# Attention sums and values as 64-row matmuls in the two column halves of the array

## Chip, cores, metric

The kernel runs on one core of one Trainium2 chip. The metric is device time in microseconds (us) from one execution, median of several. All comparisons below are between runs of the fast state; one execution of the changed kernel fell in a slow one (314.56 us at a mean granted TensorE clock of 0.982, against 0.998 to 1.0) and is left out.

## The reference

Pooled attention, then a feed-forward layer with g = h cos h. Cut to what matters:

```python
# q, k, v: (8, 8, 576, 64); keys and values are averaged over groups of 8 positions
k_p, v_p = k.reshape(B, H, 72, 8, D).mean(3), v.reshape(B, H, 72, 8, D).mean(3)
attn = np.exp(scale * q @ k_p.T - max)
out = (attn / attn.sum(-1)) @ v_p                 # (8, 8, 576, 64)
x = out.transpose(0, 2, 1, 3).reshape(4608, 512)  # tokens x (heads * 64)
h = x @ w_in                                      # 512 -> 2048
return (h * np.cos(h)) @ w_out                    # 2048 -> 512
```

## The kernel before

The feed-forward layer runs in nine stages of 512 tokens: an up stage (L297, 64 matmuls of 128x128 weights on 512 columns) and a down stage (L310, 64 more). The attention of the next batch is sprinkled into the down stage as units: scores (`scores_mm`, L211, then Exp, L218) and later values. A large unit is four heads by 256 queries, a small one (`REST`) eight heads by 64. The keys are pooled to 72, so the contraction of values and sums is over 72 rows.

```python
    banks = [psum.tile([128, 2, 512], FP32, name=f"bank{i}") for i in range(3)]     # two PSUM banks each
    obanks = [psum.tile([128, 512], FP32, name=f"obank{i}") for i in range(2)]
    ...
    def values(b, u, pair, later=None):
        (c0, n), (h0, nh) = u
        ex = att.pop(("ex", b, u))
        for i in range(nh):
            pj, hp = divmod(h0 + i, 2)
            # vz holds [v of the even head, 8s, 8s, v of the odd head], 64 columns each:
            # one matmul of 128 output rows gives values in one half and sums in the other
            nc.tensor.matmul(pair[:, hp, (i // 2) * n:(i // 2 + 1) * n],                      # L241
                             lhsT=vz[b % 2][:, pj, 2 * hp:2 * hp + 2, :].rearrange("p a d -> p (a d)"),
                             rhs=ex[:, ex_col(u, i):ex_col(u, i) + n])
        w = nh * n // 2
        lnc, inv = inverse_tile(w)
        for hp in range(2):
            nc.scalar.activation(out=lnc[half[1 - hp]], in_=pair[half[1 - hp], hp, 0:w], func=ACTF.Ln)   # L247
        nc.scalar.activation(out=inv, in_=lnc, func=ACTF.Exp, scale=-1.0)                     # L248
        def mul():
            for hp in range(2):
                nc.vector.tensor_mul(out=x_out(b, u, half[hp]), in0=cols(pair[half[hp], hp, :], u),   # L252
                                     in1=cols(inv[half[1 - hp]], u))
        ...
    # in the stage loop, for stages 1 to 6: (before which down matmul of 64, what)
            fill = [(4, scores_of((b, us[0], 2), (b, us[1], 0))), (14, V_(0, 1, later)), (16, lambda: later.pop()()),
                    (19, V_(1, 2)), (35, scores_of((b, us[2], 0), (b, us[3], 1), (t, REST, 2))),
                    (38, V_(2, 0)), (43, lambda: values(t, REST, banks[1])), (46, V_(3, 2))]
```

The prologue (batch 0) already uses `sums_first` (L266) and `values_then` (L280), which run 64-row matmuls in the column halves; the change brings that form to the steady stages.

The softmax here doesn't subtract the row's maximum and nothing guards it: scores larger than these inputs give would overflow.

## Time and profile before

| | before |
|---|---|
| time, median | 302.38 us (302.17 to 302.52, 3 runs) |
| TensorE busy | 293.9 of 301.4 us |
| ScalarE (ACT), VectorE (DVE) busy | 205.7, 170.8 us |
| one steady stage, first L297 matmul to that of the next stage | 31.30 us |

"Busy" for TensorE says little by itself, since ends of matmuls are modelled. What carries the argument is the time from the start of one group of matmuls to the start of the next, read from the timeline. The prediction below shows the lines.

### The profile page before, as it was taken

Reading aid. Unit: us, or ns where it says so; the run is one execution under the profiler, and the core shown is the slowest. Engines: PE = TensorE matmul, PEld = TensorE weight load, DVE = VectorE, ACT = ScalarE, POOL = GpSimd, SP = SyncE. Lnnn points to the kernel's source line nnn. Section 1 sums busy time; section 2 is a strip of 40 time slices with the busy share of each in tenths; the row PEclk is TensorE's granted clock in tenths of the full one; section 3 lists DMA queues with packets and bytes.
Section 4 is the critical chain, followed back from the end, with each engine's and each line's share of the span. In section 5 each row is a group of like instructions: output and inputs, shape, how many; then the busy total and the mean of one; then the engine's idle time right before and its main releaser. Section 6 shows DMA issues by size and latency. Waiting matters only on the chain.

```text
span 301.4 us, 4625 instructions
## 1 busy us (share of the span) xinstructions
PE 293.9 (97%) x1816; PEld 143.2 (48%) x1816; DVE 170.8 (57%) x212; ACT 205.7 (68%) x254; POOL 130.4 (43%) x93
## 2 busy tenths in 40 slices
PE   8789999999999999999999999999999999999995
PEld 3445544445544454445444544455444544444444
DVE  5448637465467446754666556654775477425712
ACT  3786798469876987688778886789668966605500
POOL 8463016984983398239913990389300000000000
PEclk9999999999999999999999999999999999999999
DMA  7999999639526961697079617791811130131023
GB/s 152 197 207 206 206 205 195 141 55 176 117 60 124 167 127 29 146 158 140 6 170 143 129 36 171 94 174 39 141 32 35 37 70 0 37 70 35 0 67 75
DMA packets 44165, 32.91 MB, mean 109 GB/s; under 512 B 22128, under 2 KB 39408, under 8 KB 44144
## 3 DMA queue, kind: packets, MB, share of 16 engines
q0 software_dynamic: 19744, 18.07, 38.3%
q1 hardware_dynamic: 24160, 14.42, 20.5%
q8 instruction: 14, 0.23, 0.3%
q10 hardware_dynamic: 240, 0.13, 0.2%
q14 instruction: 7, 0.06, 0.1%
HBM read 36.70 MB, written 9.44 MB: 153 GB/s over the span
## 4 chain that ended last, share of the span: by engine, by line
PE 93%; DMA 4%; POOL 1%; DVE 1%; issue 0%; POOLq 0%; DVEq 0%
PE bank L297 41%; PE obank L310 41%; PE bank L241 5%; DMA kv_st<-in_v_dram 4%; PE bank L211 3%; PE bank L328 1%; PE bank L165 1%; POOL q_b L84 1%; PE obank L157 0%; PE obank L280 0%; PE obank L192 0%; DVE xT L282 0%; DVE vz L167 0%; POOL kv_st L84 0%; DVE o_sb L316 0%
## 5 line engine op out<-in xcount | busy, mean ns | idle before, releaser
L310 PE MATMUL obank<-w_out_sb,g_sb 128*128 128x512 bf16 x560 | 131.4, 379 | 0.0
L297 PE MATMUL bank<-xT,w_in_sb 128*128 128x512 bf16 x576 | 126.6, 379 | 0.0
L304 ACT ACTIVATE cos<-bank,half_pi 128x1024 f32<-128x1024 f32 x72 | 79.3, 1113 | 59.5 <-PE bank L297 59.5
L307 DVE TENSOR_TENSOR g_sb<-bank,cos 128x1024 bf16<-128x1024 f32 x72 | 87.3, 1223 | 43.0 <-ACT cos L304 42.9
L297 PEld LDWEIGHTS <-w_in_sb 128*128 128x128 bf16 x576 | 56.1, 98 | 67.6 <-issue 1.6
L310 PEld LDWEIGHTS <-g_sb 128*128 128x128 bf16 x560 | 52.8, 98 | 56.5 <-issue 2.0
L252 DVE TENSOR_TENSOR xT<-bank,inv 64x512 bf16<-64x512 f32 (+1 forms) x72 | 45.3, 629 | 40.8 <-ACT inv L248 40.1
L141 POOL TENSOR_TENSOR kv_st<-kv_st 72x2048 f32<-72x2048 bf16 x12 | 48.7, 4058 | 33.9 <-DMA kv_st<-in_k_dram 33.9
L247 ACT ACTIVATE lnc<-bank 64x512 f32<-64x512 f32 (+1 forms) x72 | 39.2, 544 | 3.1 <-PE bank L241 1.7
L316 DVE COPY o_sb<-obank 128x512 f32<-128x512 f32 x35 | 23.6, 689 | 30.9 <-PE obank L310 30.5
L218 ACT ACTIVATE ex<-bank 72x1024 bf16<-72x1024 f32 (+1 forms) x40 | 35.0, 929 | 8.5 <-PE bank L211 8.4
L142 POOL TENSOR_TENSOR kv_st<-kv_st 72x1024 f32<-72x1024 f32 x12 | 28.2, 2349 | 1.0
L248 ACT ACTIVATE inv<-lnc 128x512 f32<-128x512 f32 (+1 forms) x36 | 21.0, 583 | 1.1
L241 PE MATMUL bank<-ex,vz 72*128 72x256 bf16 (+1 forms) x176 | 20.0, 243 | 0.0
L241 PEld LDWEIGHTS <-vz 72*128 72x128 bf16 x176 | 13.6, 97 | 9.6 <-DVE xT L252 0.5
L145 POOL TENSOR_TENSOR kp<-kv_st 72x512 bf16<-72x512 f32 x12 | 14.9, 1263 | 0.5
L211 PE MATMUL bank<-qT,kk 64*72 64x256 bf16 (+1 forms) x192 | 13.2, 252 | 0.0
L211 PEld LDWEIGHTS <-kk 64*72 64x72 bf16 x192 | 7.4, 109 | 9.9 <-issue 7.2
L285 ACT ACT_TABLE_LOAD x9 | 11.5, 1283 | 0.9 <-PEq L519 0.7
L499 POOL COPY gate<-kk 1x1 bf16<-1x1 bf16 x5 | 0.9, 179 | 25.7 <-DMA kk<-kp 25.7
L288 ACT ACT_TABLE_LOAD x9 | 11.5, 1283 | 0.2
L103 POOL DMA_DIRECT2D kv_st<-in_v_dram x6 | 5.0, 841 | 8.8 <-PE bank L165 8.8
(55 smaller groups left out, 93.1 us busy)
## 6 DMA issues: line engine op xcount, KB each, us to landing
out_dram<-o_sb SPq DMA_DIRECT2D x70, 128.0 KB, 2.4
kv_st<-in_v_dram POOLq DMA_DIRECT2D x8, 576.0 KB, 13.7
kv_st<-in_k_dram POOLq DMA_DIRECT2D x7, 576.0 KB, 7.6
q_b<-in_q_dram POOLq DMA_DIRECT2D x6, 576.0 KB, 9.9
w_in_sb<-in_moe_w_in_dram POOLq DMA_DIRECT2D x4, 512.0 KB, 14.5
w_out_sb<-in_moe_w_out_dram POOLq DMA_DIRECT2D x4, 512.0 KB, 18.1
q_b<-in_q_dram POOLq DMA_DIRECT2D x4, 288.0 KB, 13.0
g_sb<-in_k_dram SPq DMA_DIRECT2D x1, 576.0 KB, 3.7
```

The source lines that it names most:

```text
L141: add(out=s, in0=x[:, :, 0:4, :], in1=x[:, :, 4:8, :], op=ADD)
L142: add(out=s[:, :, 0:2, :], in0=s[:, :, 0:2, :], in1=s[:, :, 2:4, :], op=ADD)
L211: nc.tensor.matmul(pair[:Sp, bank, c:c + n].rearrange("p (g n) -> p g n", n=64), lhsT=kk[b % 2][half[r], h0 + i, 0:Sp], rhs=att["qT", b][h ...
L218: nc.scalar.activation(out=ex[:, 0:nh * n].rearrange("p (a n) -> p a n", a=2), in_=pair[:Sp, :, 0:nh * n // 2], func=ACTF.Exp, scale=scale ...
L241: nc.tensor.matmul(pair[:, hp, (i // 2) * n:(i // 2 + 1) * n], lhsT=vz[b % 2][:, pj, 2 * hp:2 * hp + 2, :].rearrange("p a d -> p (a d)"), ...
L247: nc.scalar.activation(out=lnc[half[1 - hp]], in_=pair[half[1 - hp], hp, 0:w], func=ACTF.Ln)
L252: nc.vector.tensor_mul(out=x_out(b, u, half[hp]), in0=cols(pair[half[hp], hp, :], u), in1=cols(inv[half[1 - hp]], u))
L297: nc.tensor.matmul(h[:, j, :], lhsT=w_in_sb[fc // 4][:, ki, (fc % 4) * 128:(fc % 4 + 1) * 128], rhs=xT[:, ki, t * TILE:(t + 1) * TILE], st ...
L304: nc.scalar.activation(out=cos, in_=h, func=ACTF.Sin, bias=half_pi[:, :1])
L307: nc.vector.tensor_mul(out=g_sb[:, 2 * fp:2 * fp + 2, :], in0=h, in1=cos)
L310: nc.tensor.matmul(o, lhsT=g_sb[:, fc, ms * 128:(ms + 1) * 128], rhs=w_out_sb[fc // 4][:, fc % 4, :], start=(fc == 0), stop=(fc == FFCH - 1))
L316: nc.vector.tensor_copy(out=o[:, 0:n], in_=ps)
```

## The change

The intent: let the sums of all heads of a unit lie in one bank over all 128 partitions and the values in the other, so that one Ln and one product over 128 partitions do what two of each over 64 did. For that, each head's matmul of 128 output rows becomes two of 64, and even and odd heads go side by side in the two column halves of the array. A stretch in which the matmuls use the divided array, between matmuls that use all of it, is called a visit below. Its way in is what the last full matmuls before it take beyond their pace, its way out what passes beyond the pace until the next full matmul starts.

```diff
-        for i in range(nh):
-            pj, hp = divmod(h0 + i, 2)
-            nc.tensor.matmul(pair[:, hp, (i // 2) * n:(i // 2 + 1) * n],
-                             lhsT=vz[b % 2][:, pj, 2 * hp:2 * hp + 2, :].rearrange("p a d -> p (a d)"),
-                             rhs=ex[:, ex_col(u, i):ex_col(u, i) + n])
         w = nh * n // 2
+        cs, ao = pair[:, 0, 0:w], pair[:, 1, 0:w]
+        for out_of, weights in ((cs, lambda i: ones[:Sp, :]),
+                                (ao, lambda i: vz[b % 2][:, (h0 + i) // 2, 3 * (i % 2), :])):
+            for i in range(nh):
+                hp = i % 2
+                nc.tensor.matmul(out_of[hp * 64:hp * 64 + 64, (i // 2) * n:(i // 2 + 1) * n], lhsT=weights(i),
+                                 rhs=ex[:, ex_col(u, i):ex_col(u, i) + n])
         lnc, inv = inverse_tile(w)
-        for hp in range(2):
-            nc.scalar.activation(out=lnc[half[1 - hp]], in_=pair[half[1 - hp], hp, 0:w], func=ACTF.Ln)
+        nc.scalar.activation(out=lnc, in_=cs, func=ACTF.Ln)
         nc.scalar.activation(out=inv, in_=lnc, func=ACTF.Exp, scale=-1.0)
 
         def mul():
-            for hp in range(2):
-                nc.vector.tensor_mul(out=x_out(b, u, half[hp]), in0=cols(pair[half[hp], hp, :], u),
-                                     in1=cols(inv[half[1 - hp]], u))
+            nc.vector.tensor_mul(out=x_out(b, u, slice(0, 128)), in0=cols(ao, u), in1=cols(inv, u))
```

## The prediction

> **What bounds the kernel now.** I read the page first: engines, slices, the chain that ended last.
>
> ```profile
> PE 293.9 (97%) x1816; PEld 143.2 (48%) x1816; DVE 170.8 (57%) x212; ACT 205.7 (68%) x254; POOL 130.4 (43%) x93
> PE 93%; DMA 4%; POOL 1%; DVE 1%; issue 0%; POOLq 0%; DVEq 0%
> ```
>
> TensorE is busy 97% of the 301.4 us span and the chain lies on it for 93%. Busy matmul time alone proves little, so I asked next whether TensorE ever waits for what the change makes cheaper: the logarithm (L247, ACT) and the products (L252, DVE). From the list of waits:
>
> ```profile
> PEld L211 <- DVE xT L252: 1.9, 7, 0.4
> ...
> PEld L241 <- DVE xT L252: 0.5, 1, 0.5
> ```
>
> (The columns are total us, times and longest.) Nobody waits for L247. The 1.9 us are seven times 0.27 us in front of the scores, and the third view shows that this is no wait for data. It is TensorE's timeline in a steady stage; the first column is the start, and I use differences of starts only, since the ends are modelled:
>
> ```profile
> 99.14 1.03 PE L310 MATMUL obank<-w_out_sb,g_sb 128*128 128x512 bf16 x4
> 100.09 0.63 PE L211 MATMUL bank<-qT,kk 64*72 64x256 bf16 x8
> 100.65 2.33 PE L310 MATMUL obank<-w_out_sb,g_sb 128*128 128x512 bf16 x10
> 102.83 0.60 PE L241 MATMUL bank<-ex,vz 72*128 72x256 bf16 x4
> 103.27 1.25 PE L310 MATMUL obank<-w_out_sb,g_sb 128*128 128x512 bf16 x5
> 104.35 0.60 PE L241 MATMUL bank<-ex,vz 72*128 72x256 bf16 x4
> ```
>
> Five L310 matmuls take 104.35 - 103.27 = 1.08 us, 0.216 each: TensorE's pace with no gap. Four of L241 take 0.44 us, 0.109 each, and the five after them lose nothing: a unit of values is free of any transition. The scores (L211), which use half arrays of 64 rows, are not: the four L310 ahead take 0.95 instead of 0.864 (0.09 lost), the eight scores in four pairs take 0.56 against 4 x 0.107 = 0.43 of streaming (0.13 lost), and the ten after them take 2.18 against 2.16 (some 0.01 to 0.02). That is 0.23 to 0.24 us per visit to a divided array. So a steady stage is TensorE's instruction stream end to end (in the chain of waits its pieces join without holes from 99.30 to 130.59), and what counts is only what the change does to that stream.
>
> **What the Trainium skill says.** "TensorEngine Tiling (Array Packing)", section Key Properties: changing the tiling mode, not merely the tile, drains TensorE. The trace agrees, with the 0.09 us in and some 0.1 us out around L211. The same page, section Restrictions under the tile-to-partition mapping: column tiling disables the fast weight load. In the trace a 72x64 weight load takes 109 ns (L280) and a 72x128 one 97 ns (L241), so the half as wide one is the slower; it overlaps matmuls all the same. "TensorE: Matmul & The Clock Gate", section Back-to-back issue gap: 262 cycles for 256 columns, 109 ns at 2.4 GHz; the trace has 0.109. "Trainium Kernel Development and Optimization", Performance Expectations, says that matmul busy time is a bad metric because matmuls are pipelined; hence the differences of starts.
>
> **The change, part by part.** `values` is used only in the loop: per batch four units of 4 heads x 256 columns for batches 1 to 7, and one of 8 heads x 64 for batches 0 to 7. That is 28 large units (112 matmuls of 256) and 8 small ones (64 of 64), as the groups by form count L241.
>
> Removed: one Ln and one product per unit.
>
> ```profile
> L252 DVE TENSOR_TENSOR xT<-bank,inv 64x512 bf16<-64x512 f32 x56 | 38.6, 689 | 38.9 <-ACT inv L248 38.4
> L247 ACT ACTIVATE lnc<-bank 64x512 f32<-64x512 f32 x56 | 33.1, 592 | 1.8 <-PE bank L241 0.7
> L252 DVE TENSOR_TENSOR xT<-bank,inv 64x256 bf16<-64x256 f32 x16 | 6.8, 422 | 1.9 <-ACT inv L248 1.6
> L247 ACT ACTIVATE lnc<-bank 64x256 f32<-64x256 f32 x16 | 6.1, 379 | 1.4 <-PE bank L241 1.0
> L282 DVE TENSOR_TENSOR xT<-obank,inv 128x512 bf16<-128x512 f32 x3 | 2.0, 688 | 0.6 <-PE obank L280 0.6
> L270 ACT ACTIVATE lnc<-obank 128x512 f32<-128x512 f32 x2 | 1.2, 597 | 0.0
> ```
>
> The last two rows, from the prologue, are the new forms: 128 partitions cost what 64 do. So ACT loses 28 x 0.592 + 8 x 0.379 = 19.6 us (205.7 to 186) and DVE 28 x 0.689 + 8 x 0.422 = 22.7 us (170.8 to 148). All of it lies beside TensorE.
>
> Added: L241's 176 matmuls become 352 of 64 output rows, two at a time in the two column halves. The prologue already runs this very form (L266, L280). Eight L280 matmuls from 16.52 to the next matmul of the same mode at 16.98 take 0.46 us, four pairs at 0.109 and 0.024 for the first pair. So the streaming of a large unit stays the same: 4 x 0.109 before, four pairs of 0.109 after. What is new is the mode, 128x64, between L310 matmuls in 128x128. Its way out is measured:
>
> ```profile
> 12.19 0.41 PE L266 MATMUL obank<-ex,ones 72*64 72x256 bf16 x4 [0.15 <-DVE kk L132]
> 12.54 0.61 PE L392 MATMUL bank<-warm 128*128 128x512 bf16 x2
> ```
>
> Two pairs to the first 128x128 matmul in 0.34 us, of which 0.213 stream: 0.13 for the first pair and the way out, the same as with L211 (four in 0.34 at 39.34 us). The way in from 128x128 never stands without a data wait in front of it; from the row mode it is 0.09 (L165's last start at 15.42, L266 at 15.61, less 0.109), as is L211's. I take 0.09.
>
> Large unit: 0.09 in + 0.13 first pair and out + 0.015 in the next matmul - 0.01 that it loses now = 0.224 us. Times 28: **6.3 us**.
>
> Small unit: now eight matmuls in 0.23 us (111.38 to 111.61). After, eight pairs of 64 columns. The nearest form is L157, 36 pairs of 72 columns in 64x64 tiles:
>
> ```profile
> 27.14 1.36 PE L157 MATMUL obank<-groups,kv_st 64*64 64x72 bf16 x72
> 28.43 0.39 PE L297 MATMUL bank<-xT,w_in_sb 128*128 128x512 bf16 x1
> ```
>
> (1.29 - 0.12) / 36 = 0.0325 us a pair. So 8 x 0.0325 + 0.12 + 0.09 + 0.015 - 0.23 = 0.25 us, times 8: **2.0 us**.
>
> Given back: in the first stage eight L310 before the values at 48.37 us take 0.20 us more than their pace, the one 0.5 us wait on L252; the shorter products should end it: -0.2. And the first small unit follows the pooling of V, whose mode change is paid already: -0.1.
>
> Sum: 302.4 + 6.3 + 2.0 - 0.3 = **310.4 us**, 2.6% slower.
>
> **The rivals.** *The relief of ACT and DVE shortens it.* For: ACT is busy about 15.7 of 17.45 us in a steady down stage, and some 42 us of work vanish. Against: no engine waits for L247, TensorE waits once for L252, and the up stage (64 matmuls in 13.85 us) runs at TensorE's own pace. At most the 0.2 us above, if entering the mode were free as well: 302.
>
> *Only half of the switch is paid*, because K stays 72 rows and the weights of the halves could be loaded ahead while the full array still streams: no 0.09 on the way in, 36 x 0.09 = 3.2 us less: 307. For: a full-width load runs ahead of the matmul in flight (the 97 ns loads cost L241 nothing). Against: L211's loads start only with its matmuls.
>
> *The two halves' weight loads do not overlap.* In the small units 16 loads in sequence at some 0.06 a pair add 8 x 8 x 0.03 = 1.8 us: 312. Against: in L157 two 64-column loads fit in 0.0325 us, though there in different rows of the array as well, which is why it stays open. In the large units 0.109 a pair hides them, as L280 shows.
>
> **Range and chances.** The 2.6% stand on one number taken 36 times, 0.22 to 0.25 us, three quarters of it measured in this form. Half a switch gives the low end with what is between, serial loads the high end: 307.9 to 312.2. The line of 2% is at 308.4; below it lies the rival with a free way in and a part of the spread. Faster by over 2%: 0.01; within 2%: 0.17; slower: 0.82.
>
> **What would show it.** In the changed profile: ACT near 186 and DVE near 148 us; no new wait of TensorE for ACT or DVE; L310 ahead of the values late by 0.09 us and the unit itself at 0.56 us instead of 0.44 to the next L310; small units near 0.38 to the next L310; up stages unchanged at 13.85 us; steady iterations longer by 4 x 0.224 + 0.25 = 1.15 us. Wrong if the L310 run ahead of the values loses nothing, if pairs start more than 0.109 us apart, or if stages shorten anywhere but at 48 us.

## The result, and the profile after

The changed kernel takes 309.8 us (median of its five executions; the four fast ones are 309.53 to 309.86, median 309.69) against 302.52 us (302.17 to 302.7, 5 runs): ratio 1.0237, 95% interval 1.0223 to 1.0252. It is slower. Ratios here and below are the mean time of one kernel's fast runs over that of the other's of the same rounds, so not quite the ratio of the medians.

The run `after_again` repeats the changed kernel on another chip and gives a fast profile:

> The changed kernel once more, for a profile of the fast state. My theory: 309.7 us as before; the profile's steady stage is 1.04 us longer than that of the kernel before, made up of five visits to the divided array at 0.22 to 0.25 us each, less 0.1 us because the scores of the last unit no longer wait for the product (L252) that frees their bank.

Measured: 309.61 us (309.33 to 309.89), ratio 1.0241 (1.0223 to 1.026). Its lines are numbered differently: L245 are the matmuls of sums and values, L248 the Ln, L249 the Exp, L252 the product, L309 the down matmuls, L296 the up matmuls. The engines on its page:

```profile
PE 300.6 (98%) x1992; PEld 141.4 (46%) x1992; DVE 148.2 (48%) x176; ACT 185.1 (60%) x218; POOL 130.4 (42%) x93
```

ACT lost 20.6 and DVE 22.6 us, as intended. TensorE's busy time grew by 6.7 us, but since ends are modelled, the starts have to say where. Its timeline in a steady stage (columns: start, length, engine, line, operation):

```profile
99.99 1.03 PE L309 MATMUL obank<-w_out_sb,g_sb 128*128 128x512 bf16 x4
100.95 0.63 PE L211 MATMUL bank<-qT,kk 64*72 64x256 bf16 x8
101.51 2.33 PE L309 MATMUL obank<-w_out_sb,g_sb 128*128 128x512 bf16 x10
103.77 0.41 PE L245 MATMUL bank<-ex,ones 72*64 72x256 bf16 x4
104.01 0.39 PE L245 MATMUL bank<-ex,vz 72*64 72x256 bf16 x4
104.33 1.25 PE L309 MATMUL obank<-w_out_sb,g_sb 128*128 128x512 bf16 x5
105.51 0.41 PE L245 MATMUL bank<-ex,ones 72*64 72x256 bf16 x4
```

Ten L309 now take 2.26 instead of 2.18 us, which is the way in (0.08), and five take 1.18 instead of 1.08, the way in of the next visit and 0.01 to 0.02 left from the one before. The unit itself takes 0.56 from its start (103.77) to the next L309 (104.33) instead of 0.44. The weight-load row shows the same from the other side. In the list of waits (us in total, times, longest):

```profile
PEld L245 <- issue: 15.0, 36, 0.4
```

Thirty-six units, and in front of each the weight loads stand still for some 0.4 us: the first load for the divided array starts with the unit's first matmul (both at 103.77 us) and not ahead of it. L241's loads, before, were idle this way 0.2 us once.

Where the time went, by stages of these two profiles (each from the first up matmul to the next stage's, or in the first stage from the first down matmul; precise starts of the trace):

| | before | changed | difference | predicted |
|---|---|---|---|---|
| down stage 0 | 19.37 | 20.54, of it 0.36 waiting for the load of w_out | 0.80 without that wait | 0.85 |
| stages 1 to 6, each | 31.297 | 32.330 | 1.033, times 6: 6.20 | 1.15, times 6: 6.9 |
| stage 7 (one small unit) | 28.258 | 28.498 | 0.24 | 0.25 |
| stage 8 and the end | 31.40 | 31.39 | 0.0 | 0.0 |

Without that wait the stages lose 7.2 us together; the medians differ by 7.3.

The 0.36 us are a matter of the start: that execution reached its first up matmul 1.34 us earlier than the one of before (17.04 against 18.38 us) and so came to a weight matrix that was still on its way (the timeline names the load of w_out as what ended the wait). Such differences of the start move whole times by some tenths from execution to execution, which is why I compare stages where less than 1 us is at stake.

### The profile page after: what moved, and what is told of

It is laid out like the page before. It is cut to its first block, busy times and chain, and to the rows that moved or that the text cites. A ratio compares the mean times of both kernels' runs of the same rounds, so it can differ in the third digit from the quotient of the medians.

```text
span 312.8 us, 4899 instructions
## 1 busy us (share of the span) xinstructions
PE 304.6 (97%) x1992; PEld 142.7 (46%) x1992; DVE 148.2 (47%) x176; ACT 185.3 (59%) x218; POOL 130.5 (42%) x93
## 4 chain that ended last, share of the span: by engine, by line
PE 93%; DMA 3%; POOL 1%; issue 1%; DVE 0%; ACT 0%; POOLq 0%
PE bank L296 41%; PE obank L309 40%; PE bank L245 6%; DMA kv_st<-in_v_dram 3%; PE bank L211 3%; PE bank L327 1%; PE obank L279 1%; POOL q_b L84 1%; PE obank L157 0%; PE bank L165 0%; PE obank L192 0%; ACT ex L218 0%; DVE vz L167 0%; POOL kv_st L84 0%; PE bank L265 0%
## 5 line engine op out<-in xcount | busy, mean ns | idle before, releaser
L309 PE MATMUL obank<-w_out_sb,g_sb 128*128 128x512 bf16 x560 | 131.7, 380 | 0.0
L296 PE MATMUL bank<-xT,w_in_sb 128*128 128x512 bf16 x576 | 128.9, 384 | 0.0
L296 PEld LDWEIGHTS <-w_in_sb 128*128 128x128 bf16 x576 | 56.6, 99 | 69.5 <-issue 4.8
L309 PEld LDWEIGHTS <-g_sb 128*128 128x128 bf16 x560 | 50.4, 98 | 61.7 <-issue 7.5
L252 DVE TENSOR_TENSOR xT<-bank,inv 128x512 bf16<-128x512 f32 (+1 forms) x36 | 22.8, 632 | 43.5 <-ACT inv L249 43.1
L248 ACT ACTIVATE lnc<-bank 128x512 f32<-128x512 f32 (+1 forms) x36 | 19.8, 549 | 8.8 <-PE bank L245 8.4
L249 ACT ACTIVATE inv<-lnc 128x512 f32<-128x512 f32 (+1 forms) x36 | 21.0, 583 | 1.1
L245 PE MATMUL bank<-ex,ones 72*64 72x256 bf16 (+1 forms) x176 | 14.0, 253 | 0.0
L245 PE MATMUL bank<-ex,vz 72*64 72x256 bf16 (+1 forms) x176 | 13.3, 245 | 0.0
L245 PEld LDWEIGHTS <-ones 72*64 72x64 bf16 x176 | 6.0, 108 | 15.0 <-issue 15.0
L211 PE MATMUL bank<-qT,kk 64*72 64x256 bf16 (+1 forms) x192 | 12.1, 250 | 0.0
L211 PEld LDWEIGHTS <-kk 64*72 64x72 bf16 x192 | 7.9, 110 | 8.5 <-issue 7.6
```

The lines of the kernel that those rows point to most:

```text
L211: nc.tensor.matmul(pair[:Sp, bank, c:c + n].rearrange("p (g n) -> p g n", n=64), lhsT=kk[b % 2][half[r], h0 + i, 0:Sp], rhs=att["qT", b][h ...
L245: nc.tensor.matmul(out_of[hp * 64:hp * 64 + 64, (i // 2) * n:(i // 2 + 1) * n], lhsT=weights(i), rhs=ex[:, ex_col(u, i):ex_col(u, i) + n])
L252: nc.vector.tensor_mul(out=x_out(b, u, slice(0, 128)), in0=cols(ao, u), in1=cols(inv, u))
L296: nc.tensor.matmul(h[:, j, :], lhsT=w_in_sb[fc // 4][:, ki, (fc % 4) * 128:(fc % 4 + 1) * 128], rhs=xT[:, ki, t * TILE:(t + 1) * TILE], st ...
L309: nc.tensor.matmul(o, lhsT=g_sb[:, fc, ms * 128:(ms + 1) * 128], rhs=w_out_sb[fc // 4][:, fc % 4, :], start=(fc == 0), stop=(fc == FFCH - 1))
```

## The experiments

**The two halves of the change, each alone.** `pe_part` makes the same number and shapes of matmuls, in pairs in the column halves, but with the old layout of banks (each pair is now the sums and the values of one head), so ACT and DVE do the old work:

```diff
-            nc.tensor.matmul(pair[:, hp, (i // 2) * n:(i // 2 + 1) * n],
-                             lhsT=vz[b % 2][:, pj, 2 * hp:2 * hp + 2, :].rearrange("p a d -> p (a d)"),
-                             rhs=ex[:, ex_col(u, i):ex_col(u, i) + n])
+            for a in range(2):
+                nc.tensor.matmul(pair[half[a], hp, (i // 2) * n:(i // 2 + 1) * n],
+                                 lhsT=vz[b % 2][:, pj, 2 * hp + a, :], rhs=ex[:, ex_col(u, i):ex_col(u, i) + n])
```

> TensorE's half of the change alone: 64-row matmuls in column halves, but laid out in the banks as before, so that two Ln and two products per unit remain. Theory (the cost is the visits): the same TensorE stream as the changed kernel, 309.5 to 310.5 us; the relief of ACT and DVE is worth at most 0.1 us a stage. Rival (the lighter ACT and DVE hide a larger TensorE cost in the changed kernel): over 312 us.

Measured: 309.26 us (309.22 to 309.37), just under the range expected, ratio 1.023 (1.0213 to 1.0248); steady stages of 32.33 us, equal to the changed kernel's. TensorE's half is the whole of the loss.

`relief_part` keeps the 128-row matmuls and takes one Ln and one product per unit. For that the weights are chosen so that the first bank holds sums in all partitions and the second values. Its output is wrong, which doesn't matter for the time.

```diff
-                             lhsT=vz[b % 2][:, pj, 2 * hp:2 * hp + 2, :].rearrange("p a d -> p (a d)"),
+                             lhsT=weights(pj, hp),        # 128 neighbouring columns of vz
...
-        for hp in range(2):
-            nc.scalar.activation(out=lnc[half[1 - hp]], in_=pair[half[1 - hp], hp, 0:w], func=ACTF.Ln)
+        nc.scalar.activation(out=lnc, in_=pair[:, 0, 0:w], func=ACTF.Ln)
...
-            for hp in range(2):
-                nc.vector.tensor_mul(out=x_out(b, u, half[hp]), in0=cols(pair[half[hp], hp, :], u),
-                                     in1=cols(inv[half[1 - hp]], u))
+            nc.vector.tensor_mul(out=x_out(b, u, slice(0, 128)), in0=cols(pair[:, 1, :], u), in1=cols(inv, u))
```

> The other half alone, wrong results on purpose: TensorE's matmuls of 128 output rows as before, but one Ln and one product per unit over 128 partitions. Theory: only the wait of the last scores for L252 goes (0.14 us in some six stages), of which 0.08 comes back as a wait for the exponential: 301.6 us, 0.2 to 0.4% faster. Rival (ACT and DVE hold TensorE up more than the waits show): below 300 us; rival (nothing at all is to be had): 302.5.

Measured: 301.96 us (301.69 to 303.09), ratio 0.9993 (0.9973 to 1.0013). The steady stage is 31.292 us against 31.297: the relief is worth nothing there. My expectation, 0.14 us a stage with 0.08 of it coming back, was wrong, and the timelines say why. The kernel before, second scores of a stage and what follows, and ACT at the same time:

```profile
108.34 0.93 PE L211 MATMUL bank<-qT,kk 64*72 64x256 bf16 x16
109.20 0.82 PE L310 MATMUL obank<-w_out_sb,g_sb 128*128 128x512 bf16 x3
109.86 0.27 PE L241 MATMUL bank<-ex,vz 72*128 72x256 bf16 x1
108.79 1.93 ACT L218 ACTIVATE ex<-bank 72x1024 bf16<-72x1024 f32 x2 [1.32 <-PE bank L211]
```

The same in `relief_part` (L312 are its down matmuls, L246 its values):

```profile
107.43 0.76 PE L211 MATMUL bank<-qT,kk 64*72 64x256 bf16 x16
108.12 0.82 PE L312 MATMUL obank<-w_out_sb,g_sb 128*128 128x512 bf16 x3
108.95 0.60 PE L246 MATMUL bank<-ex,vz 72*128 72x256 bf16 x4
107.88 1.93 ACT L218 ACTIVATE ex<-bank 72x1024 bf16<-72x1024 f32 x2 [2.48 <-PE bank L211]
```

The sixteen scores take 0.69 instead of 0.86 us to the next group: a wait of 0.17 us for L252, in front of the last eight of them, is indeed gone. But the three down matmuls now take 0.83 instead of 0.66, and the values start 1.52 us after the scores in both. They need the first exponential of those scores (the ACT line holds two, about 1 us each). It starts 0.45 us after the scores in both kernels, once the first eight are done, and so ends just before the values start. One wait lay beside another that ends at the same moment.

**What a unit pays for.** `split_visit` puts one down matmul between the sums and the values of each unit: the same instructions, twice as many visits to the divided array.

```diff
                                 (ao, lambda i: vz[b % 2][:, (h0 + i) // 2, 3 * (i % 2), :])):
+            if out_of is ao and between is not None:
+                between()
             for i in range(nh):
...              # between puts the next down matmul; the stage loop is changed to match
```

> The changed kernel with one output-projection matmul between the sums and the values of each unit: the same instructions, but two visits to the divided array per unit instead of one. Theory (each visit costs 0.22 us, in, first pair and out): 36 x 0.225 = 8.1 us more than the changed kernel, 317.8 us. Rival (the cost comes with the doubled number of matmuls and the slower weight loads): no change, 309.7 us.

Measured: 317.71 us (317.26 to 318.6), ratio 1.0513 (1.049 to 1.0536): 8.1 us above the changed kernel, 0.225 us for each of the 36 added visits. Its timeline (L311 are the down matmuls, L247 the sums and values):

```profile
105.79 0.41 PE L247 MATMUL bank<-ex,ones 72*64 72x256 bf16 x4
106.14 0.39 PE L311 MATMUL obank<-w_out_sb,g_sb 128*128 128x512 bf16 x1
106.45 0.41 PE L247 MATMUL bank<-ex,vz 72*64 72x256 bf16 x4
106.80 0.39 PE L311 MATMUL obank<-w_out_sb,g_sb 128*128 128x512 bf16 x1
```

Two pairs take 0.34 to the next L311 where 0.22 would be their pace, and one L311 takes 0.32 (precise starts) to the next group instead of 0.216: 0.22 to 0.23 for an added visit.

`tiny_visit` is the kernel before with one small pair of 64-row matmuls ahead of each unit:

```diff
         ex = att.pop(("ex", b, u))
+        for a in range(2):
+            nc.tensor.matmul(pair[half[a], 0, 0:64], lhsT=ones[:Sp, :], rhs=ex[:, 0:64])
         for i in range(nh):
```

> The kernel before with one pair of 64-column matmuls in the column halves, whose result is overwritten, ahead of the four or eight matmuls of each unit. All else is as before. Theory (a visit costs the same however little is done in it): 36 x 0.23 = 8.3 us more, less up to 0.9 us as the wait for L252 is covered: 309.9 to 310.8 us. Rival (cost by matmuls and weight loads): 72 small ones, 36 x 0.03 = 1.1 us more, 303.6 us.

Measured: 311.13 us (310.54 to 311.21), ratio 1.0282 (1.0261 to 1.0302), a little over the range expected. In the profiled execution (311.18 us) that excess is not of the visits: the stretch from the last matmul to the end is 4.51 us, against 3.72 before. No visit lies there, and why it was longer was not looked into. A pair that streams for 0.03 us costs as much as the whole change: its steady stages are 32.467 us, 1.17 above those of before, for five visits. The lines (L240 the pair, L243 the old matmuls, L312 the down matmuls):

```profile
103.99 0.22 PE L240 MATMUL bank<-ex,ones 72*64 72x64 bf16 x2
104.14 0.61 PE L243 MATMUL bank<-ex,vz 72*128 72x256 bf16 x4
104.59 1.25 PE L312 MATMUL obank<-w_out_sb,g_sb 128*128 128x512 bf16 x5
105.76 0.22 PE L240 MATMUL bank<-ex,ones 72*64 72x64 bf16 x2
```

0.15 us from the pair to the next matmul, 0.45 for the four old ones, 1.17 instead of 1.08 for the five down matmuls ahead of the next visit.

`grouped` goes the other way: the changed kernel with two visits per steady stage instead of five.

```diff
-            fill = [(4, scores_of(...)), (14, V_(0, 1, later)), (16, lambda: later.pop()()),
-                    (19, V_(1, 2)), (35, scores_of(...)),
-                    (38, V_(2, 0)), (43, lambda: values(t, REST, banks[1])), (46, V_(3, 2))]
+            fill = [(4, scores_of(...)), (19, V_(0, 1)), (19, V_(1, 2)), (35, scores_of(...)),
+                    (43, V_(2, 0)), (43, V_(3, 2)), (43, lambda: values(t, REST, banks[1]))]
```

> The changed kernel with the units of six steady stages gathered into two visits per stage instead of five (two units at the nineteenth matmul, two and the small one at the forty-third). Theory: three visits fewer in six stages, 18 x 0.224 = 4.0 us less than the changed kernel: 305.7 us, still slower than the kernel before. If the products at the stage's end come too late for the next stage, up to 0.5 us a stage comes back: up to 308.7. Rival (cost by matmuls): 309.7 us.

Measured: 305.22 us (304.28 to 305.79), ratio 1.0089 (1.0072 to 1.0107); stages of 31.57 us, 0.76 less than the changed kernel's for three visits fewer (18 visits, 4.6 us by stages, 4.4 by times of different chips). Three visits at 0.22 are 0.67; the other 0.09 is about the wait for the exponential in front of the third unit, which now comes later (the three L309 there take 0.83 in the changed kernel and 0.75 elsewhere). No product was late for the stage's end. It is the best form of the changed kernel that I ran, and still 0.9% slower than the kernel before.

**Do the halves share their time?** `halves_in_turn` was to show it by order: all matmuls of one half ahead of all of the other.

```diff
-        for out_of, weights in ((cs, ...), (ao, ...)):
-            for i in range(nh):
-                hp = i % 2
+        for hp in range(2):
+            for out_of, weights, i in [(o, f, i) for o, f in ((cs, ...), (ao, ...)) for i in range(hp, nh, 2)]:
```

> The changed kernel with all matmuls of one column half ahead of all of the other, so that only one pair in a unit can run side by side. Theory (pairs share their time): a large unit takes seven slots of 0.108 us instead of four, +0.325 us x 28 = 9.1, a small one fifteen of about 0.03 instead of eight, +0.2 us x 8 = 1.7: 320.5 us. Rival (the halves do not overlap anyway, or the order does not matter): 309.7 us.

Measured: 310.83 us (310.6 to 311.42), ratio 1.0281 (1.0263 to 1.0299): 1.2 us above the changed kernel and not 11. The expectation missed, and not because pairs gain nothing. A small unit of it, where the program has four sums and four values of the first half, then four sums and four values of the second:

```profile
113.79 0.31 PE L244 MATMUL bank<-ex,ones 72*64 72x64 bf16 x4
113.94 0.20 PE L244 MATMUL bank<-ex,vz 72*64 72x64 bf16 x1
113.94 0.22 PE L244 MATMUL bank<-ex,ones 72*64 72x64 bf16 x1
113.97 0.20 PE L244 MATMUL bank<-ex,vz 72*64 72x64 bf16 x1
114.00 0.20 PE L244 MATMUL bank<-ex,ones 72*64 72x64 bf16 x1
```

The sums of the second half start between the values of the first: they overtake matmuls that stand ahead of them in the program. The unit takes 0.524 us to the next down matmul instead of 0.374, while a large unit, with only four matmuls in a half, takes 0.570 instead of 0.560. So in this trace each half takes its matmuls in its own order, some three or four ahead, and the order of the program mattered only beyond that. 28 x 0.01 + 8 x 0.15 = 1.5 us is about what was measured.

`one_half` tests the same by place: all matmuls of a unit in the lower half. Its output is wrong, which doesn't matter for the time.

```diff
-                nc.tensor.matmul(out_of[hp * 64:hp * 64 + 64, (i // 2) * n:(i // 2 + 1) * n], lhsT=weights(i),
+                nc.tensor.matmul(out_of[half[0], (i // 2) * n:(i // 2 + 1) * n], lhsT=weights(i),
...              # Ln and Exp on half[0] alone; two products, both from half[0]
```

> The changed kernel with all of a unit's 64-row matmuls in the lower column half, wrong results on purpose; Ln, Exp and products read that half alone. It replaces the test by order, which failed because the two halves took their matmuls independently of each other. Theory (two halves share their time, one cannot): eight slots of 0.108 us instead of four in a large unit, +0.43 us x 28 = 12.1, sixteen of 0.0315 instead of eight in a small one, +0.25 us x 8 = 2.0: 309.6 + 14.1 = 323.7 us. Rival (the halves gave nothing): 309.6 us.

Measured: 323.24 us (323.16 to 323.69), ratio 1.0696 (1.0673 to 1.0718). Its unit (L310 are the down matmuls) is 0.99 us from start to the next down matmul, against 0.56:

```profile
107.57 0.63 PE L245 MATMUL bank<-ex,ones 72*64 72x256 bf16 x4
108.03 0.60 PE L245 MATMUL bank<-ex,vz 72*64 72x256 bf16 x4
108.56 0.61 PE L310 MATMUL obank<-w_out_sb,g_sb 128*128 128x512 bf16 x2
```

The halves do share their time, 0.43 us a large unit. The change needs that only to break even with the 128-row form, which fills all columns by itself.

**Can the two waits found be turned into time?** In the kernel before, `before_later` moves the second scores and all that follows by one down matmul, so the bank is free when the scores come.

```diff
-                    (19, V_(1, 2)), (35, scores_of((b, us[2], 0), (b, us[3], 1), (t, REST, 2))),
-                    (38, V_(2, 0)), (43, lambda: values(t, REST, banks[1])), (46, V_(3, 2))]
+                    (19, V_(1, 2)), (36, scores_of((b, us[2], 0), (b, us[3], 1), (t, REST, 2))),
+                    (39, V_(2, 0)), (44, lambda: values(t, REST, banks[1])), (47, V_(3, 2))]
```

> The kernel before with the second scores and the values that follow moved back by one output-projection matmul in six stages, so that the bank which they need is free when they come. Theory: the wait of 0.14 us for L252 in these stages goes, 302.5 - 0.8 = 301.7 us, 0.3% faster. Rival (it moves elsewhere or was no wait): 302.5 us.

Measured: 302.06 us (301.83 to 302.58), ratio 0.9989 (0.9975 to 1.0004), stages 31.290 us: nothing, for the reason found in `relief_part`. `before_v2_later` moves the third unit of values by two (40 instead of 38, the rest as above):

```diff
-                    (39, V_(2, 0)), ...
+                    (40, V_(2, 0)), ...
```

> The kernel before with the second scores one output-projection matmul later (as in the run that moved all by one) and the values that follow them two later, so that they wait neither for the product that frees the bank nor for their exponential. What the traces so far show: these values start 1.522 us after their scores in every version, held by the exponential; so taking away the wait of 0.17 us for L252 alone gave nothing. Theory: with both gone, six stages lose 0.17 us each: 302.5 - 1.0 = 301.5 us, ratio 0.9967. Rival (a third wait, or the values are then late for the stage's end): 302.4 us or more.

Measured: 301.82 us (301.4 to 302.08), ratio 0.9983 (0.9967 to 1.0). The steady stages are 31.167 us, 0.13 below those of before in each of six, so the stages themselves are shorter by 0.8 us; of the 0.17 expected, 0.04 came back in front of the small unit of values. In the whole time this gain is at the edge of what the runs resolve: call it same, at best 0.2%.

## Why the prediction was right

It said 310.4 us, in a range of 307.9 to 312.2, slower by over 2%; measured 309.8. By its steps:

- *TensorE's stream sets the end, and the relief of ACT and DVE lies beside it.* Shown: `pe_part` loses as much as the whole change, `relief_part` gains nothing in steady stages. The 0.2 us that it did grant, in front of the values in stage 0, came true: the eight down matmuls there took 1.93 us before and 1.83 after, with 0.09 of way in now included; `relief_part`'s stage 0 is 0.21 us shorter than that of before. But the shorter products were not needed for it: in `pe_part`, with the old products, these eight take 1.83 us as well; TensorE comes there later, after the visits before, and presumably finds the old product done.
- *The streaming of a large unit stays the same.* Shown: four pairs at 0.109 us, and `one_half` for what it would be without pairs.
- *Each visit costs 0.224 us.* Shown three ways: 0.225 by `split_visit`, 0.22 by the timeline, and about as much by `tiny_visit` for next to no work. The way in from the full array, which no line of before showed without a data wait, is 0.08 to 0.09, as assumed; the rival of half a switch is out.
- *A small unit takes 0.38 us.* 0.374; its pairs start 0.0315 apart, so the rival of weight loads in sequence is out.
- *The 0.27 us in front of the scores are no wait for data.* This step was wrong for the second scores of a stage. The line shown in the prediction is of the first scores, which have no such wait; six of the seven waits counted, 0.24 us each in the weight loads, stand in the middle of the second scores, and there 0.17 us of TensorE's time was a wait for L252. That it did no harm to the sum was luck: that wait lay beside the wait for the exponential.
- *Five visits lengthen a stage by 1.15 us.* 1.033. The term mis-sized is the third large unit's way in: 0.09 that I added to the path lies in the slack between scores and values (1.52 us apart in both kernels), because the scores no longer wait. (They do not in `pe_part` either: its list of waits has none of L211 for L252, presumably because TensorE comes later.) That is 0.09 of the 0.12 a stage, and with it most of the 0.6 us between forecast and result; the rest is a few hundredths of rounding in my terms.

Three slips in the working did not matter to the result. Of the 0.224 us a visit, 0.13 to 0.145 had been measured between column halves and the full array, not three quarters. 8 x 8 x 0.03 is 1.9 and not 1.8. And the rival of half a switch, at 307, lies below the range whose low end it is said to give.

## What to carry to other kernels

In this kernel dividing the array cost 0.22 us per visit, however many matmuls the visit held: count how often the stream of matmuls goes from full to divided and back, multiply by what a neighbouring divided group already loses in the timeline, and compare it with what the other engines' relief is worth on the path, which here was 0.2 us in one stage and nothing in the others. A matmul that pads its output rows with something useful (here the sums beside the values) fills the full array and paid no visit here. And before a wait is counted as a gain, look whether the next thing in the stream is held by something else until the same moment.

## What the Trainium skill lacked or had wrong

- "TensorEngine Tiling (Array Packing)", Key Properties, says that a change of mode drains TensorE and gives no figure. Here a visit to 128x64 from 128x128 costs 0.22 us at full clock: 0.08 to 0.09 in, 0.02 on the first pair, 0.1 out, 0.01 on the first full matmul after (0.225 by `split_visit`). One to 64x128 (L211) costs 0.23 to 0.24.
- "TensorE: Matmul & The Clock Gate", The mechanism in Part 3, says that matmuls start and end strictly in program order. In `halves_in_turn` matmuls of the second column half start before ones of the first that stand ahead of them (at 113.94 us, between values that the program puts first). Whether a semaphore on the last matmul is then always the last to fire no run here tests.
